# Grouped-query attention and a squared-ReLU FFN on one core: transposes moved from TensorE to DMA crossbar transposes

## The chip, the cores and the metric

The kernel runs on one core of a Trainium2 chip. The metric is the device time of one execution in microseconds (us), lower is better; the median of several runs is compared.

## The reference

Eight batches of attention with 16 query heads over 4 key/value heads (sequence 384, head size 64), then an FFN with a squared ReLU on the 3072 rows that come out:

```python
batch, n_q_heads, n_kv_heads, seq, head_dim = (8, 16, 4, 384, 64)
n_tokens, d_model, d_ff = (3072, 1024, 2048)
k = np.repeat(k, group, axis=1); v = np.repeat(v, group, axis=1)
scores = scale * np.matmul(q, k.transpose(0, 1, 3, 2))
attn = np.exp(scores - max); attn = attn / (np.sum(attn) + 1e-09)
x = np.matmul(attn, v).transpose(0, 2, 1, 3).reshape(B * S, H * D)
h = np.maximum(x @ w_in, 0.0)
out = (h * h @ w_out)
```

## The kernel before

Inputs are loaded as bf16 by POOL's DMA queue, one batch of k, v and q at a time, some two batches ahead; the FFN weights stay in SBUF. A batch has 8 pairs of heads (`NPB`), and p counts pairs over all batches, 64 in all. TensorE contracts over partitions, so q and k (which arrive with the sequence on partitions) must be turned to have the head size there, and the attention output must be turned to have the model dimension there. The kernel before does all of this on TensorE with an identity matrix, three 128x128 transposes to a group, into one PSUM buffer `pt`, which DVE copies out:

- `emit_kT(gi)` (L243): one group for each key head; k has first been doubled by a DVE copy (`emit_k`, into `k_dup`) so that two heads of a pair can use the two halves of the array.
- `emit_qT(p)` (L256): one group for each pair.
- `emit_oT(p)` (L308): one group for each pair, from `o_sb` into chunk c of `xT`, the FFN's input.

All four engines get their instructions from a recorder in the order in which the `emit_` functions are called; it works out the semaphore waits from what each operation reads and writes. Each engine runs its own list in order.

That order is a loop over steps n. A step does the scores of pair n (`emit_sc`, three times: two matmuls on halves of the array, then exp on ACT), the product with v of pair n-1 (`emit_av`, nine matmuls twice), its normalisation on DVE (`emit_norm`: reciprocal, multiply into `o_sb`), the kT and qT groups of pair n+2 and the oT group of pair n-1. Between these it calls `fill(ns)`, which takes FFN blocks of four matmuls from a generator until a credit is used up. The FFN of batch b may start once its last oT is recorded (`done_x`), so batch 0's attention runs without FFN work; from then on a batch's FFN has slightly more work than the slots of a batch take, so it falls back further with each batch, and the last FFN runs alone at the end. An FFN of a batch is 16 tiles of 8 up matmuls of 384 columns (L332; relu on DVE into `hr`, Square on ACT into `h2T`), then 6 tiles of 16 down matmuls of 512 columns (L352; copy on DVE into `y_sb`, store by SP's queue). The first half of an up tile reads chunks 0 to 3 of `xT`, the second chunks 4 to 7.

Of the kernel before, what the change touches and what calls it, by code (L numbers as in the profile page):

```python
# [5 lines left out]
ALU = mybir.AluOpType  # L6
# [4 lines left out]
class Recorder:  # L11
# [6 lines left out]
    def __init__(self, nc):  # L18
        self.nc = nc
        self.ops = []  # L20
        self.writer = {}
        self.readers = {}
        self.dma_sems = {}

    def add(self, eng, fn, reads=(), writes=(), dma=None):
        i = len(self.ops)
        deps = set()
        for r in reads:
            if r in self.writer:
                deps.add(self.writer[r])  # L30
        for w in writes:
            if w in self.writer:
                deps.add(self.writer[w])
            deps.update(self.readers.get(w, ()))
        raw = {self.writer[r] for r in reads if r in self.writer}
        for r in reads:
            self.readers.setdefault(r, []).append(i)
        for w in writes:
            self.writer[w] = i
            self.readers[w] = []  # L40
        need = set()
        for d in deps:
            o = self.ops[d]
            if o["dma"] is None and o["eng"] == eng and dma is None:
                if eng in self.IN_ORDER or d not in raw:
                    continue
            need.add(d)
        self.ops.append(dict(eng=eng, fn=fn, dma=dma, need=need, signal=False))
        return i

# [54 lines left out]
def bass_gqa_attention__then__ffn_squared_relu_kernel(  # L105
# [11 lines left out]
    B, H, S, D = 8, 16, 384, 64  # L117
    HKV = 4
    NJ = S // 128
    FF = 2048  # L120
    F = H * D
    NPB = H // 2
    NP = B * NPB
    NKC = F // 128
    NFC = FF // 128
    NST, NQT, NKT, NEX, NXT, NHR, NY = 3, 3, 2, 3, 3, 3, 3

    R = Recorder(nc)

    def sb(name, shape, dt=bf16):  # L130
        return nc.alloc_sbuf_tensor(name, shape, dt)

    ident = sb("ident", [128, 128])
    warm = sb("warm", [128, 512])
    q_st = [sb(f"q_st{i}", [128, H, NJ * D]) for i in range(NST)]
    k_st = [sb(f"k_st{i}", [128, HKV, NJ, D]) for i in range(NST)]
    k_dup = [sb(f"k_dup{i}", [128, HKV * NJ, 2, D]) for i in range(2)]
    v_st = [sb(f"v_st{i}", [128, HKV * NJ, D]) for i in range(NST)]
    v_aug = [sb(f"v_aug{i}", [128, HKV * NJ, D + 1]) for i in range(2)]
    kT = [sb(f"kT{i}", [128, S]) for i in range(NKT)]  # L140
    qT = [sb(f"qT{i}", [128, S]) for i in range(NQT)]
    expT = [sb(f"expT{i}", [128, NJ, 2 * S]) for i in range(NEX)]
    rinv = [sb(f"rinv{i}", [128, NJ, 2], f32) for i in range(2)]
    o_sb = [sb(f"o_sb{i}", [128, NJ, 2, D]) for i in range(2)]
    xT = [sb(f"xT{i}", [128, NKC, S]) for i in range(NXT)]
    w_in_sb = sb("w_in_sb", [128, NKC, FF])
    w_out_sb = sb("w_out_sb", [128, NFC, F])
# [4 lines left out]
    sc_ps = [nc.alloc_psum_tensor(f"sc_ps{i}", [128, 2, 512], f32) for i in range(2)]  # L152
    po = nc.alloc_psum_tensor("po", [128, 512], f32)
    pt = nc.alloc_psum_tensor("pt", [128, 1024], bf16)
    f_ps = [nc.alloc_psum_tensor(f"f_ps{i}", [128, 512], f32) for i in range(2)]
    po_v = po[:, 0:NJ * 2 * (D + 1)].rearrange("p (i s e) -> p i s e", i=NJ, s=2)


    def load_k(b):
        st = b % NST  # L160
        R.add("gpsimd", lambda g: g.dma_start(
            k_st[st].ap().rearrange("p g j d -> p g (j d)"),
            k[b].rearrange("g (p j) d -> p g (j d)", j=NJ)),
            writes=[("k_st", st)], dma=f"k{st}")
# [68 lines left out]
    def emit_v(b):  # L233
        R.add("vector", lambda e: e.tensor_copy(v_aug[b % 2][:, :, 0:D], v_st[b % NST][:, :, :]),
              reads=[("v_st", b % NST)], writes=[("v_aug", b % 2)])

    def emit_k(b):
        src = k_st[b % NST].ap().rearrange("p g j d -> p (g j) d").unsqueeze(2)
        R.add("vector", lambda e: e.tensor_copy(  # L239
            k_dup[b % 2][:, :, :, :], src.to_broadcast([128, HKV * NJ, 2, D])),  # L240
            reads=[("k_st", b % NST)], writes=[("k_dup", b % 2)])

    def emit_kT(gi):  # L243
        b, g = gi // HKV, gi % HKV

        def tr(pe):
            for j in range(NJ):
                src = k_dup[b % 2][:, g * NJ + j].rearrange("p x d -> p (x d)")
                m = pe.matmul(pt[:, j * 128:(j + 1) * 128], src, ident[:], is_transpose=True)  # L249
            return m  # L250

        R.add("tensor", tr, reads=[("k_dup", b % 2), "ident"], writes=["pt"])
        R.add("vector", lambda e: e.tensor_copy(kT[gi % NKT][:, :], pt[:, 0:S]),  # L253
              reads=["pt"], writes=[("kT", gi % NKT)])

    def emit_qT(p):  # L256
        b, c = p // NPB, p % NPB
        st = b % NST
        src = q_st[st][:, 2 * c:2 * c + 2, :].rearrange("p h e -> p (h e)")

        def tr(pe):
            for t in range(NJ):
                m = pe.matmul(pt[:, t * 128:(t + 1) * 128], src[:, t * 128:(t + 1) * 128], ident[:],  # L263
                              is_transpose=True)
            return m

        R.add("tensor", tr, reads=[("q_st", st, 2 * c), ("q_st", st, 2 * c + 1), "ident"], writes=["pt"])
        R.add("vector", lambda e: e.tensor_copy(qT[p % NQT][:, :], pt[:, 0:S]),  # L268
              reads=["pt"], writes=[("qT", p % NQT)])

    def emit_sc(p, j):
        gi, u = p // 2, (p * NJ + j) % 2

        def sc(pe):
            for x in range(2):
                rows = slice(64 * x, 64 * x + 64)
                m = pe.matmul(sc_ps[u][:, x, 0:S], kT[gi % NKT][rows, j * 128:(j + 1) * 128],  # L277
                              qT[p % NQT][rows, :])
            return m

        R.add("tensor", sc, reads=[("kT", gi % NKT), ("qT", p % NQT)], writes=[("sc", u)])
        src = sc_ps[u][:, :, 0:S].rearrange("p x (t c) -> p x t c", t=NJ)
        dst = expT[p % NEX][:, j, :].rearrange("p (t x c) -> p x t c", x=2, t=NJ)
        R.add("scalar", lambda e: e.activation(dst, src, AF.Exp, scale=0.125),  # L284
              reads=[("sc", u)], writes=[("expT", p % NEX, j)])
# [15 lines left out]
    def emit_norm(p):  # L301
        R.add("vector", lambda e: e.reciprocal(rinv[p % 2].ap().unsqueeze(3), po_v[:, :, :, D:D + 1]),  # L302
              reads=["po"], writes=[("rinv", p % 2)])
        rb = rinv[p % 2].ap().unsqueeze(3).to_broadcast([128, NJ, 2, D])
        R.add("vector", lambda e: e.tensor_tensor(o_sb[p % 2][:, :, :, :], po_v[:, :, :, 0:D], rb, ALU.mult),  # L305
              reads=["po", ("rinv", p % 2)], writes=[("o_sb", p % 2)])

    def emit_oT(p):  # L308
        b, c = p // NPB, p % NPB

        def tr(pe):
            for i in range(NJ):
                m = pe.matmul(pt[:, i * 128:(i + 1) * 128],  # L313
                              o_sb[p % 2][:, i].rearrange("p s d -> p (s d)"), ident[:], is_transpose=True)
            return m

        R.add("tensor", tr, reads=[("o_sb", p % 2), "ident"], writes=["pt"])
        R.add("vector", lambda e: e.tensor_copy(xT[b % NXT][:, c, :], pt[:, 0:S]),  # L318
              reads=["pt"], writes=[("xT", b % NXT, c)])

# [60 lines left out]
    def fill(ns):  # L381
        credit[0] += ns
        while credit[0] > 0:
            t = next(ffn, 0)
            if not t:
                credit[0] = 0.0
                return
            credit[0] -= t

    emit_k(0)  # L390
    emit_v(0)
    emit_kT(0)
    emit_qT(0)
    emit_qT(1)
    SLOT = 4900 / 7.0
    for n in range(NP + 2):
        live = n < NP
        if live:
            emit_sc(n, 0)
            fill(SLOT)  # L400
            emit_sc(n, 1)
            fill(SLOT)
        if 0 <= n - 1 < NP:
            emit_av(n - 1, 0)
            fill(SLOT)
            emit_av(n - 1, 1)
            emit_norm(n - 1)
            fill(SLOT)
        if live:
            emit_sc(n, 2)  # L410
            fill(SLOT)
        if n + 2 < NP:
            if (n + 2) % NPB == 0:
                bn = (n + 2) // NPB
                emit_k(bn)
                emit_v(bn)
                if bn + 2 < B:
                    load_k(bn + 2)
                    load_v(bn + 2)
                    load_q(bn + 2, 0)  # L420
            if (n + 2) % 2 == 0:
                emit_kT((n + 2) // 2)
                fill(SLOT / 2)
            emit_qT(n + 2)
            fill(SLOT)
        if 0 <= n - 1 < NP:
            emit_oT(n - 1)
            fill(SLOT)
            if n % NPB == 0:
                done_x[0] = n // NPB - 1  # L430
# [32 lines left out]
```

## Time and profile before

| | us |
|---|---|
| median of 3 runs | 517.85 (517.54 to 524.07) |
| the profiled execution | 519.5 |
| its span, first to last instruction | 517.7 |
| PE busy in it | 487.7 |
| DVE busy | 209.4 |
| ACT busy | 213.6 |

PE is TensorE's matmul stream, PEld its weight loads, DVE, ACT, POOL and SP the other engines. Matmuls overlap in the pipeline, so their mean duration is longer than the time that each adds; the chain of work that ended last counts from end to end. Times within the span count from its first instruction.

### The profile page before, as it was taken

To read this page: it belongs to the slowest core of one execution; us is meant where nothing else is said; L and a number is where in the kernel's file an instruction comes from. 1 tells how busy PE (TensorE), PEld (TensorE's weight loads), DVE (VectorE), ACT (ScalarE), POOL (GpSimd) and SP (SyncE) were. 2 spreads that over 40 slices of the span, in tenths; PEclk is the share of its full clock that TensorE was granted. 3 is DMA by queue.
4 is the path that set the end of the run, shared out by engine and by line. 5 is a ranking of instruction groups with operands and counts; after the bars stand their busy time and mean duration, and the time that the engine had idled before them with its cause. 6 is when DMAs were issued, how large, how long until landed. Compare 5 with 4: busy or idle time off the path is not lost.

```text
span 517.7 us, 8710 instructions
## 1 busy us (share of the span) xinstructions
PE 487.7 (94%) x3832; PEld 247.7 (48%) x3832; DVE 209.4 (40%) x483; ACT 213.6 (41%) x321; POOL 32.6 (6%) x43
## 2 busy tenths in 40 slices
PE   6879998999989999999999999989999999999997
PEld 3434554455534554445544545444554445545643
DVE  2443444345433444434443445324443344433421
ACT  2654552345532555335543355333553345601410
POOL 8720002000010000100000000000000000000000
PEclk8776999999999999999999999999999999999999
DMA  9999997310091001810051100011001110011012
GB/s 117 196 198 207 207 126 105 70 42 0 1 133 63 20 1 17 138 42 22 1 82 44 61 0 1 30 53 42 0 2 42 42 41 1 2 62 61 1 42 81
DMA packets 42358, 30.97 MB, mean 60 GB/s; under 512 B 25936, under 2 KB 34128, under 8 KB 42320
## 3 DMA queue, kind: packets, MB, share of 16 engines
q0 software_dynamic: 35408, 17.83, 26.4%
q1 hardware_dynamic: 6912, 12.59, 6.3%
q8 instruction: 30, 0.49, 0.4%
q14 instruction: 8, 0.07, 0.0%
HBM read 35.65 MB, written 12.58 MB: 93 GB/s over the span
## 4 chain that ended last, share of the span: by engine, by line
PE 90%; DVE 7%; issue 1%; DMA 1%; POOL 0%; ACT 0%; POOLq 0%
PE f_ps L332 33%; PE f_ps L352 33%; PE sc_ps L277 10%; PE po L294 8%; PE pt L313 3%; PE pt L263 3%; DVE hr L339 2%; DVE qT L268 2%; DVE kT L253 1%; PE pt L249 1%; DVE y_sb L360 1%; DVE o_sb L305 1%; DMA v_st<-in_v_dram 1%; DVE k_dup L239 0%; DVE rinv L302 0%
## 5 line engine op out<-in xcount | busy, mean ns | idle before, releaser
L284 ACT ACTIVATE expT<-sc_ps 128x768 bf16<-128x768 f32 x192 | 150.5, 804 | 149.4 <-PE sc_ps L277 148.9
L332 PE MATMUL f_ps<-xT,w_in_sb 128*128 128x384 bf16 x1024 | 203.6, 329 | 0.0
L352 PE MATMUL f_ps<-w_out_sb,h2T 128*128 128x512 bf16 x768 | 191.5, 380 | 0.0
L341 ACT ACTIVATE h2T<-hr 128x384 bf16<-128x384 f32 x128 | 66.9, 523 | 131.3 <-DVE hr L339 129.0
L332 PEld LDWEIGHTS f_ps<-xT,w_in_sb 128*128 128x128 bf16 x1024 | 86.5, 98 | 55.6 <-issue 13.8
L339 DVE TENSOR_SCALAR hr<-f_ps 128x384 f32<-128x384 f32 x128 | 71.2, 556 | 88.5 <-PE f_ps L332 88.5
L352 PEld LDWEIGHTS f_ps<-w_out_sb,h2T 128*128 128x128 bf16 x768 | 65.0, 97 | 66.2 <-issue 11.0
L360 DVE COPY y_sb<-f_ps 128x512 f32<-128x512 f32 x48 | 33.2, 692 | 84.2 <-PE f_ps L352 83.8
L277 PE MATMUL sc_ps<-qT,kT 64*128 64x384 bf16 x384 | 65.1, 348 | 0.9 <-ACT expT L284 0.6
L294 PEld LDWEIGHTS po<-v_aug,expT 128*128 128x128 bf16 x1152 | 52.2, 100 | 22.7 <-issue 4.7
L294 PE MATMUL po<-v_aug,expT 128*128 128x65 bf16 x1152 | 57.1, 197 | 0.0
L277 PEld LDWEIGHTS sc_ps<-qT,kT 64*128 64x128 bf16 x384 | 17.6, 94 | 59.0 <-issue 45.1
L302 DVE RECIPROCAL rinv<-po 128x6 f32<-128x6 f32 x64 | 12.4, 193 | 60.9 <-PE po L294 60.9
L305 DVE TENSOR_TENSOR o_sb<-po,rinv 128x384 bf16<-128x384 f32 x64 | 35.7, 557 | 2.2
L263 PE MATMUL pt<-ident,q_st 128*128 128x128 bf16 x192 | 22.3, 227 | 13.3 <-DVE kT L253 12.9
L318 DVE COPY xT<-pt 128x384 bf16<-128x384 bf16 x64 | 22.7, 355 | 24.7 <-PE pt L313 24.7
L268 DVE COPY qT<-pt 128x384 bf16<-128x384 bf16 x64 | 22.7, 355 | 24.6 <-PE pt L263 24.4
L313 PE MATMUL pt<-ident,o_sb 128*128 128x128 bf16 x192 | 22.1, 226 | 8.4 <-DVE qT L268 7.0
L263 PEld LDWEIGHTS pt<-ident,q_st 128*128 128x128 bf16 x192 | 13.8, 99 | 25.4 <-DVE kT L253 17.9
L313 PEld LDWEIGHTS pt<-ident,o_sb 128*128 128x128 bf16 x192 | 12.9, 99 | 25.0 <-DVE qT L268 20.1
L178 POOL DMA_DIRECT2D q_st<-in_q_dram x9 | 10.0, 1115 | 209.8 <-PE pt L263 209.8
L253 DVE COPY kT<-pt 128x384 bf16<-128x384 bf16 x32 | 11.4, 356 | 14.2 <-PE pt L249 14.0
(19 smaller groups left out, 60.7 us busy)
## 6 DMA issues: line engine op xcount, KB each, us to landing
out_dram<-y_sb SPq DMA_DIRECT2D x48, 256.0 KB, 2.0
q_st<-in_q_dram POOLq DMA_DIRECT2D x7, 768.0 KB, 9.8
w_in_sb<-in_moe_w_in_dram POOLq DMA_DIRECT2D x8, 512.0 KB, 17.8
w_out_sb<-in_moe_w_out_dram POOLq DMA_DIRECT2D x4, 1024.0 KB, 38.5
k_st<-in_k_dram POOLq DMA_DIRECT2D x8, 192.0 KB, 10.7
v_st<-in_v_dram POOLq DMA_DIRECT2D x8, 192.0 KB, 11.0
q_st<-in_q_dram POOLq DMA_DIRECT2D x1, 576.0 KB, 8.1
q_st<-in_q_dram POOLq DMA_DIRECT2D x1, 192.0 KB, 4.1
```

Of the source, the lines that this page charges most:

```text
L263: m = pe.matmul(pt[:, t * 128:(t + 1) * 128], src[:, t * 128:(t + 1) * 128], ident[:], is_transpose=True)
L268: R.add("vector", lambda e: e.tensor_copy(qT[p % NQT][:, :], pt[:, 0:S]), reads=["pt"], writes=[("qT", p % NQT)])
L277: m = pe.matmul(sc_ps[u][:, x, 0:S], kT[gi % NKT][rows, j * 128:(j + 1) * 128], qT[p % NQT][rows, :])
L284: R.add("scalar", lambda e: e.activation(dst, src, AF.Exp, scale=0.125), reads=[("sc", u)], writes=[("expT", p % NEX, j)])
L294: m = pe.matmul(po_v[:, i, s, :], expT[p % NEX][:, j, f * 128:(f + 1) * 128], v_aug[b % 2][:, g * NJ + j, :], start=(j == 0), stop=(j == N ...
L305: R.add("vector", lambda e: e.tensor_tensor(o_sb[p % 2][:, :, :, :], po_v[:, :, :, 0:D], rb, ALU.mult), reads=["po", ("rinv", p % 2)], wri ...
L313: m = pe.matmul(pt[:, i * 128:(i + 1) * 128], o_sb[p % 2][:, i].rearrange("p s d -> p (s d)"), ident[:], is_transpose=True)
L332: m = pe.matmul(f_ps[u][:, 0:S], w_in_sb[:, kc, c * 128:(c + 1) * 128], xT[b % NXT][:, kc, :], start=(kc == 0), stop=(kc == NKC - 1))
L339: R.add("vector", lambda e, u=u, r=r: e.tensor_scalar_max(hr[r][:, :], f_ps[u][:, 0:S], 0.0), reads=[("f_ps", u)], writes=[("hr", r)])
L341: R.add("scalar", lambda e, r=r, c=c: e.activation(h2T[b % 2][:, c, :], hr[r][:, :], AF.Square), reads=[("hr", r)], writes=[("h2T", b % 2, ...
L352: m = pe.matmul(f_ps[u][:, :], h2T[b % 2][:, c, i * 128:(i + 1) * 128], w_out_sb[:, c, jj * 512:(jj + 1) * 512], start=(c == 0), stop=(c = ...
L360: R.add("vector", lambda e, u=u, yb=yb, jj=jj: e.tensor_copy(y_sb[yb][:, jj * 512:(jj + 1) * 512], f_ps[u][:, :]), reads=[("f_ps", u)], wr ...
```

## The change

From batch 2 on (`DMA_QK = 2`) q and k, and from batch 1 on (`DMA_O = 1`) the attention output, are turned by DMA crossbar transposes issued by SP, from SBUF to SBUF, in place of TensorE groups and DVE copies. For each batch one transpose turns the whole of `k_dup` (128x1536) into `kTb`, and two turn the halves of `q_st` (128x1536 each) into `qTb`; they are issued in step n = 8b - 5, with the k copy, which moves there from step 8b - 2. Each pair's `o_sb` (128x384) is turned into its chunk of `xT` by a transpose recorded where the oT group was; `o_sb` has four buffers in place of two. A DMA also waits for the last one with the same semaphore. For batch 1 the v copy now stands ahead of the k copy. The calls of `fill` stay as they are.

```diff
+        if dma is not None:
+            if dma in self.dma_last:
+                need.add(self.dma_last[dma])
+            self.dma_last[dma] = i
...
+    DMA_QK, DMA_O = 2, 1
+    NST, NQT, NKT, NEX, NXT, NHR, NY, NO = 3, 3, 2, 3, 3, 3, 3, 4
...
+    qTb = [sb(f"qTb{i}", [128, NPB, S]) for i in range(2)]
+    kTb = [sb(f"kTb{i}", [128, HKV, S]) for i in range(2)]
...
+    def emit_turn(b):
+        R.add("sync", lambda e: e.dma_start_transpose(
+            kTb[b % 2].ap().rearrange("p g (j c) -> p (g j) c", j=NJ),
+            k_dup[b % 2].ap().rearrange("p a x d -> p (a x d)")),
+            reads=[("k_dup", b % 2)], writes=[("kTb", b % 2)], dma=f"kt{b % 2}")
+        for part in range(2):
+            cs = slice(4 * part, 4 * part + 4)
+            R.add("sync", lambda e, cs=cs: e.dma_start_transpose(
+                qTb[b % 2][:, cs, :].rearrange("p h (t c) -> p (h t) c", t=NJ),
+                q_st[b % NST][:, 2 * cs.start:2 * cs.stop, :].rearrange("p h e -> p (h e)")),
+                reads=[("q_st", b % NST, h) for h in range(2 * cs.start, 2 * cs.stop)],
+                writes=[("qTb", b % 2, part)], dma=f"qt{b % 2}_{part}")
...
     def emit_kT(gi):
         b, g = gi // HKV, gi % HKV
+        if b >= DMA_QK:
+            return
...
     def emit_qT(p):
         b, c = p // NPB, p % NPB
+        if b >= DMA_QK:
+            return
...
+        if b >= DMA_QK:
+            kt, kt_key = kTb[b % 2][:, c // 2, :], ("kTb", b % 2)
+            qt, qt_key = qTb[b % 2][:, c, :], ("qTb", b % 2, c // 4)
...
     def emit_oT(p):
         b, c = p // NPB, p % NPB
+        if b >= DMA_O:
+            R.add("sync", lambda e: e.dma_start_transpose(
+                xT[b % NXT][:, c, :].rearrange("p (i c) -> p i c", i=NJ),
+                o_sb[p % NO].ap().rearrange("p i s d -> p (i s d)")),
+                reads=[("o_sb", p % NO)], writes=[("xT", b % NXT, c)], dma=f"xt{p % 8}")
+            return
...
         if n + 2 < NP:
+            if (n + 5) % NPB == 0 and n + 5 >= DMA_QK * NPB:
+                emit_k((n + 5) // NPB)
+                emit_turn((n + 5) // NPB)
             if (n + 2) % NPB == 0:
                 bn = (n + 2) // NPB
-                emit_k(bn)
                 emit_v(bn)
+                if bn < DMA_QK:
+                    emit_k(bn)
```

## Rows read from the trace of the kernel before

**Rows 1.** The page: engines' busy time, and the granted clock in 40 slices.

```profile
PE 487.7 (94%) x3832; PEld 247.7 (48%) x3832; DVE 209.4 (40%) x483; ACT 213.6 (41%) x321; POOL 32.6 (6%) x43
...
PEclk8776999999999999999999999999999999999999
```

**Rows 2.** The page: the chain that ended last, by line.

```profile
PE f_ps L332 33%; PE f_ps L352 33%; PE sc_ps L277 10%; PE po L294 8%; PE pt L313 3%; PE pt L263 3%; DVE hr L339 2%; DVE qT L268 2%; DVE kT L253 1%; PE pt L249 1%; DVE y_sb L360 1%; DVE o_sb L305 1%; DMA v_st<-in_v_dram 1%; DVE k_dup L239 0%; DVE rinv L302 0%
```

**Rows 3.** The chain in order of time, 200 to 232: start, us, what.

```profile
202.40 0.17 PE pt L263 x3
202.56 0.86 PE f_ps L352 x4
...
203.60 0.27 PE sc_ps L277 x2
203.87 0.97 PE f_ps L352 x4
...
206.07 0.28 PE po L294 x9
...
225.25 0.34 PE pt L313 x3
```

**Rows 4.** The chain in order of time, 455 us to the end.

```profile
459.25 13.81 PE f_ps L352 x64
473.06 20.80 PE f_ps L332 x128
```

**Rows 5.** Groups of PE, 107 to 459: count, busy us, mean ns, idle before.

```profile
L332 PE MATMUL f_ps<-xT,w_in_sb 128*128 128x384 bf16 x768 | 155.1, 327 | 0.0
L352 PE MATMUL f_ps<-w_out_sb,h2T 128*128 128x512 bf16 x515 | 132.7, 380 | 0.0
L277 PE MATMUL sc_ps<-qT,kT 64*128 64x384 bf16 x280 | 46.4, 333 | 0.0
L294 PE MATMUL po<-v_aug,expT 128*128 128x65 bf16 x864 | 42.4, 194 | 0.0
L313 PE MATMUL pt<-ident,o_sb 128*128 128x128 bf16 x143 | 16.0, 221 | 3.2 <-DVE qT L268 2.0
L263 PE MATMUL pt<-ident,q_st 128*128 128x128 bf16 x135 | 15.0, 220 | 7.5 <-DVE kT L253 7.5
L249 PE MATMUL pt<-ident,k_dup 128*128 128x128 bf16 x66 | 7.3, 220 | 1.7 <-DVE k_dup L239 1.7
```

**Rows 6.** Groups of PE, 50.3 to 107.

```profile
L352 PE MATMUL f_ps<-w_out_sb,h2T 128*128 128x512 bf16 x95 | 24.5, 380 | 0.0
L332 PE MATMUL f_ps<-xT,w_in_sb 128*128 128x384 bf16 x104 | 21.1, 327 | 0.0
L277 PE MATMUL sc_ps<-qT,kT 64*128 64x384 bf16 x44 | 7.4, 333 | 0.0
L294 PE MATMUL po<-v_aug,expT 128*128 128x65 bf16 x126 | 6.1, 194 | 0.0
L313 PE MATMUL pt<-ident,o_sb 128*128 128x128 bf16 x24 | 2.7, 221 | 1.5 <-DVE qT L268 1.3
```

**Rows 7.** Groups by line, whole span: the v copy.

```profile
L234 DVE COPY v_aug<-v_st 128x768 bf16<-128x768 bf16 x8 | 2.9, 359 | 2.1 <-DMA v_st<-in_v_dram 2.1
```

**Rows 8.** The page: SP's DMA queue (packets, MB, share), its issues (us to landing).

```profile
q1 hardware_dynamic: 6912, 12.59, 6.3%
...
out_dram<-y_sb SPq DMA_DIRECT2D x48, 256.0 KB, 2.0
```

**Rows 9.** The q loads: POOL's timeline (batch 2's issue), and landing times.

```profile
17.98 1.29 POOL L178 DMA_DIRECT2D q_st<-in_q_dram  x1
...
DMA to landing us min/median/max: 4.1/8.6/43.3
```

**Rows 10.** The timeline, 100 to 109: start, us, engine, what.

```profile
101.62 0.56 DVE L305 TENSOR_TENSOR o_sb<-po,rinv 128x384 bf16<-128x384 f32 x1
...
108.69 0.49 PE L332 MATMUL f_ps<-xT,w_in_sb 128*128 128x384 bf16 x2
```

More of the change, by code (lines that the diff above doesn't have):

```diff
@@ L23, in __init__ @@
         self.dma_sems = {}
+        self.dma_last = {}
     def add(self, eng, fn, reads=(), writes=(), dma=None):
@@ L125, in bass_gqa_attention__then__ffn_squared_relu_kernel @@
     NFC = FF // 128
-    NST, NQT, NKT, NEX, NXT, NHR, NY = 3, 3, 2, 3, 3, 3, 3
+    DMA_QK, DMA_O = 2, 1
+    NST, NQT, NKT, NEX, NXT, NHR, NY, NO = 3, 3, 2, 3, 3, 3, 3, 4
     R = Recorder(nc)
@@ L141, in bass_gqa_attention__then__ffn_squared_relu_kernel @@
     qT = [sb(f"qT{i}", [128, S]) for i in range(NQT)]
+    qTb = [sb(f"qTb{i}", [128, NPB, S]) for i in range(2)]
+    kTb = [sb(f"kTb{i}", [128, HKV, S]) for i in range(2)]
     expT = [sb(f"expT{i}", [128, NJ, 2 * S]) for i in range(NEX)]
     rinv = [sb(f"rinv{i}", [128, NJ, 2], f32) for i in range(2)]
-    o_sb = [sb(f"o_sb{i}", [128, NJ, 2, D]) for i in range(2)]
+    o_sb = [sb(f"o_sb{i}", [128, NJ, 2, D]) for i in range(NO)]
     xT = [sb(f"xT{i}", [128, NKC, S]) for i in range(NXT)]
@@ L272, in emit_sc @@
         gi, u = p // 2, (p * NJ + j) % 2
+        b, c = p // NPB, p % NPB
+        if b >= DMA_QK:
+            kt, kt_key = kTb[b % 2][:, c // 2, :], ("kTb", b % 2)
+            qt, qt_key = qTb[b % 2][:, c, :], ("qTb", b % 2, c // 4)
+        else:
+            kt, kt_key = kT[gi % NKT], ("kT", gi % NKT)
+            qt, qt_key = qT[p % NQT], ("qT", p % NQT)
         def sc(pe):
@@ L276, in sc @@
                 rows = slice(64 * x, 64 * x + 64)
-                m = pe.matmul(sc_ps[u][:, x, 0:S], kT[gi % NKT][rows, j * 128:(j + 1) * 128],
-                              qT[p % NQT][rows, :])
+                m = pe.matmul(sc_ps[u][:, x, 0:S], kt[rows, j * 128:(j + 1) * 128], qt[rows, :])
             return m
-        R.add("tensor", sc, reads=[("kT", gi % NKT), ("qT", p % NQT)], writes=[("sc", u)])
+        R.add("tensor", sc, reads=[kt_key, qt_key], writes=[("sc", u)])
         src = sc_ps[u][:, :, 0:S].rearrange("p x (t c) -> p x t c", t=NJ)
@@ L304, in emit_norm @@
         rb = rinv[p % 2].ap().unsqueeze(3).to_broadcast([128, NJ, 2, D])
-        R.add("vector", lambda e: e.tensor_tensor(o_sb[p % 2][:, :, :, :], po_v[:, :, :, 0:D], rb, ALU.mult),
-              reads=["po", ("rinv", p % 2)], writes=[("o_sb", p % 2)])
+        R.add("vector", lambda e: e.tensor_tensor(o_sb[p % NO][:, :, :, :], po_v[:, :, :, 0:D], rb, ALU.mult),
+              reads=["po", ("rinv", p % 2)], writes=[("o_sb", p % NO)])
     def emit_oT(p):
         b, c = p // NPB, p % NPB
+        if b >= DMA_O:
[4 more added lines that the diff above has]
+            return
         def tr(pe):
@@ L313, in tr @@
                 m = pe.matmul(pt[:, i * 128:(i + 1) * 128],
-                              o_sb[p % 2][:, i].rearrange("p s d -> p (s d)"), ident[:], is_transpose=True)
+                              o_sb[p % NO][:, i].rearrange("p s d -> p (s d)"), ident[:], is_transpose=True)
             return m
-        R.add("tensor", tr, reads=[("o_sb", p % 2), "ident"], writes=["pt"])
+        R.add("tensor", tr, reads=[("o_sb", p % NO), "ident"], writes=["pt"])
         R.add("vector", lambda e: e.tensor_copy(xT[b % NXT][:, c, :], pt[:, 0:S]),
```

## The prediction

> **What bounds the kernel now.** The page comes first: PE is busy for 94% of the span, DVE for 40%, ACT for 41%, and the clock row stays at 9 from the seventh slice to the end [rows 1]. Next the chain of work that ended last, by line: the two FFN matmul lines carry two thirds of it, scores and attention-times-values 18%, and the three transpose lines (L249, L263, L313) with the DVE copies that empty `pt` most of what is left [rows 2]. So whatever is taken out of PE's own order moves the end, and work on other engines counts only where PE waits for it.
>
> Then the chain piece by piece in a steady stretch, for unit prices measured end to end (the mean of one matmul on the page contains its pipeline latency and must not be multiplied) [rows 3]: three transposes between two FFN blocks 0.17 us; a pair of score matmuls 0.27; nine value matmuls 0.28; four FFN matmuls 0.86 after a transpose or a value group, but 0.97 after scores, so scores cost 0.27 + 0.11 = 0.38. The row at 225.25 shows the other side of a transpose: with no FFN block before it the group takes 0.34, because `pt` is one buffer and its DVE copy must end first. The pure FFN at the end gives the remaining units, with nothing else in the way [rows 4]: 20.80 / 128 = 0.1625 us for an up matmul, 13.81 / 64 = 0.216 for a down matmul.
>
> Last, counts of each kind in the two stretches that the change touches, with the idle time ahead of each [rows 5, 6]. All of PE's idle time from 107 to 459 us stands ahead of transposes: 3.2 + 7.5 + 1.7 = 12.4 us.
>
> **What is removed.** By the loop, TensorE loses 8 x 6 = 48 qT groups, 4 x 6 = 24 kT groups and 8 x 7 = 56 oT groups, three transposes each: 128 of 160 groups. DVE loses as many copies.
>
> *107 to 459 us* (here every transpose goes): the other work is 768 x 0.1625 + 515 x 0.216 + 140 x 0.38 + 96 x 0.28 = 124.8 + 111.2 + 53.2 + 26.9 = 316.1 us [rows 3 to 5]. The stretch lasts 352.0, so transposes and what they make PE wait for cost **35.9 us**. A cross-check: 344 transposes are 115 groups, 115 x 0.17 = 19.5; idle 12.4; the remaining 4 is the pipeline running empty before each wait (the 0.34 against 0.17).
>
> *50.3 to 107 us* (steps 9 to 16, 56.7 us): 104 x 0.1625 + 95 x 0.216 + 22 x 0.38 + 14 x 0.28 = 49.7 us, so 7.0 us of excess [rows 3, 4, 6]. Here qT(12) to qT(15), kT(6) and kT(7) stay on PE: 6 x 0.17 = 1.0, and a stall in the two steps that have a kT; (35.9 - 19.5) / 48 steps = 0.34 a step, so 0.7. Saved: 7.0 - 1.7 = **5.3 us**. After 459 us only FFN is left [rows 4]; before 50 us nothing is removed.
>
> **What is added or moved on the engines.** For batch 1 `emit_v` now comes ahead of `emit_k`, in a stretch where the chain runs through the kT transpose: one v copy later, **0.36 us** lost [rows 7]. For batches 2 to 7 the k copy runs three steps earlier on a DVE that is idle over half of the time. The slots between attention steps are still filled by the same calls, so PE's order of the remaining work is unchanged.
>
> **What is added on SP and the DMA engines.** Per batch three transposes of 128x1536 and eight of 128x384: 36 + 24 = 60 blocks of 128x128. No row shows a crossbar transpose. Below: the store on the same queue moves 256 KB and lands in 2.0 us [rows 8], so 32 KB at its rate take 0.25 us. Above, if each source row of 256 bytes is one packet: the SP queue's 6912 packets took 6.3% of 16 engines' 517.7 us, 75 ns each [rows 8]; 128 x 75 ns / 16 = 0.6 us a block. Further off, a whole landing of 2.0 us for each block (the slow rival). A gain below zero is not possible from an added transfer. I take 0.25 to 0.6, since the store is on the same queue: 15 to 36 us of the queue in a batch. PE's new batch is 316.1 / 48 x 8 = 52.7 us, so the queue keeps up, and its price on the path is nothing as long as three covers hold:
>
> - The q and k transposes of batch b are issued in step 8b-5 and first read in step 8b: 5 steps of 6.6 us (316.1 / 48) = 33 us. 36 blocks at 0.6 and the 15 blocks of the oT issued in between are 31 us: tight at the upper bound only. For batch 2 the issue is at about 50.3 + 2 x 7.1 = 64.5 us; its q load was issued at 18 us and no q load took over 43.3 us to land [rows 9], so it is there by 61.
> - The last oT of batch 1: `o_sb` is ready at 101.62 + 0.56 = 102.2 us, and the FFN half that reads chunks 4 to 7 starts at 108.69 [rows 10]: 6.5 us, some 5.5 with PE's gains in between. Three blocks at 0.6 plus 2.0 for landing are 3.8 us. Later batches have more room, since the FFN falls further behind. If this cover fails, PE stands still at the head of the FFN for the difference, at most seven times.
> - SP issues in order. Queued behind a waiting transpose are the y stores (three `y_sb` buffers, each filled again a batch later) and the next oT; DVE's `norm` now waits for the transpose of four steps before, 26 us. POOL's q loads wait for crossbar transposes in place of PE's, a batch ahead of use.
>
> With the stalls on `pt` gone, what is late next is PE itself: ACT is busy 41% of the span and DVE 40% [rows 1], and DVE loses copies.
>
> [...]
>
> **The sum.** 35.9 + 5.3 - 0.4 = 40.8 us. The profiled execution took 519.5 us (span 517.7, 1.8 around it): 478.7 after. It stood 1.65 us above the median of 517.85, so the forecast for the median is **477 us**, -7.9%.
>
> **Rivals.**
> *The stalls move instead of going* (the DVE copies that PE waited for queue behind `hr` and `y_sb` copies and `norm`; exp or Square may take their place). Only the groups' own time is then won: 128 x 0.17 = 21.8, **496 us**. For it: `hr`, `norm` and exp still empty the banks that PE fills. Against: all of PE's idle is ahead of transposes [rows 5], and each score and FFN bank has a second buffer.
> *The crossbar is the bound, slower than before.* One queue turns one block at a time, c us each. It keeps up to c = 52.7 / 60 = 0.88. Beyond, from 64.5 us on it has 15 blocks of batch 1, 6 x 36 for q and k and 6 x 24 for oT: 375, and behind the last the final FFN, 20.8 + 96 x 0.216 = 41.5 us, and a store's 2.0: the end is at 108 + 375c. That passes the time before at c = 1.09; at a store's full landing per block, 2.0, it is **858 us**. For it: nothing shown excludes a serial crossbar. Against: stores of 128 rows of 2 KB land whole in those 2.0 us.
> [...]
>
> **Chances and range.** All stalls gone 0.78 (own range 472 to 487: a few us at the FFN heads, or units that come out a little better); stalls move 0.13; crossbar the bound 0.07 (slower); a gain mostly eaten by late landings 0.02 (no change). Two per cent is about what a measurement of this kernel can tell from no change, and both first cases are beyond it: faster 0.91, same 0.02, slower 0.07. The range 471 to 491 leaves out the slow rival and most of the second.
>
> **What would show it.** No idle time on PE after about 90 us; transposes of q and k landing well ahead of step 8b; the FFN's first half following the previous batch's last store at once; SP's time from `o_sb` to landing under 5 us; PE's pieces 0.86 and 0.97 unchanged (a slower one would mean that crossbar traffic disturbs PE's reads). Wrong it would be by a wait of PE for `kTb`, `qTb` or `xT`, or DVE waiting at L305 for a transpose.

## The result, and the profile after

The changed kernel takes 478.9 us at the median (477.49 to 481.75), the kernel before 520.96 in the runs beside it: a ratio of 0.920, 95% interval 0.910 to 0.929. The forecast was 477, range 471 to 491. The profiled execution has a span of 475.7 us against 517.7; the forecast for the span was 476.9.

Up to the first FFN tile (steps 0 to 8, where the kernels do nearly the same) the granted TensorE clock is 0.50 of full speed for a varying share of the time (in the kernel before its mean is 0.51 from 10 to 20 us, 1.00 from 20 to 30 and 0.67 from 30 to 40; with only the output by crossbar 0.54, 0.50 and 0.50), so that stretch takes 37 to 48 us by chance and design together; profiles are therefore compared below from the first FFN up matmul to the end of the span. That matmul is here, in the profile before and in the one after (timeline: start, us, engine, what; line numbers are those of each kernel's own file):

```profile
43.03 2.74 PE L332 MATMUL f_ps<-xT,w_in_sb 128*128 128x384 bf16 x8
43.50 2.74 PE L369 MATMUL f_ps<-xT,w_in_sb 128*128 128x384 bf16 x8
```

So 475.7 - 43.5 = 432.2 us are left after it; in the kernel before 517.7 - 43.0 = 474.7.

Where did 42.5 us go? Between the starts of the FFN's batches (first up matmul of each, from the same timeline): batch 0 to 1 took 64.7 us and takes 58.9; batch 1 to 6 took 310.3 and takes 277.4; from there to the end 99.7 and 95.9. The gain is spread over all batches that still have attention, and nothing is given back at the end.

The groups of PE in the steady part, 107 to 420 us (count, busy us, mean ns, idle before), answer to [rows 5]:

```profile
L369 PE MATMUL f_ps<-xT,w_in_sb 128*128 128x384 bf16 x752 | 143.3, 327 | 0.0
L389 PE MATMUL f_ps<-w_out_sb,h2T 128*128 128x512 bf16 x504 | 126.4, 380 | 1.8 <-issue 0.9
L309 PE MATMUL sc_ps<-qTb,kTb 64*128 64x384 bf16 x276 | 45.7, 332 | 0.0
L325 PE MATMUL po<-v_aug,expT 128*128 128x65 bf16 x846 | 41.5, 194 | 0.0
```

The transposes are gone from the list, and with them the idle time. The 1.8 us at L389 are not a wait: this profile lacks the records of some matmuls (504 of L389 against 527 weight loads in the same stretch). A second profile of the same kernel ("changed, again" below) has them, and its row has no idle time:

```profile
L389 PE MATMUL f_ps<-w_out_sb,h2T 128*128 128x512 bf16 x526 | 129.5, 380 | 0.0
```

By the unit prices of [rows 3, 4] its work is 751 x 0.1625 + 526 x 0.216 + 138 x 0.38 + 94 x 0.28 = 314.4 us, in a stretch of 313: within half a per cent, nothing else is left. The kernel before had 316 in 352. PE's pieces are unchanged as well: from 200 to 215 us four FFN matmuls take 0.86 us, or 0.97 after scores, as before.

What PE waited for in the whole span (us in total, times, longest):

```profile
PE pt L288 <- DVE kT L276: 4.5, 6, 2.2
PE pt L350 <- DVE qT L293: 3.6, 8, 0.5
PE f_ps L389 <- issue: 1.3, 8, 0.2
PE pt L272 <- DVE k_dup L247: 1.2, 1, 1.2
...
PE f_ps L369 <- DMA xT<-o_sb: 0.6, 1, 0.6
```

The rows with `pt` are batches 0 and 1, which still turn on TensorE; the row with "issue" is the missing records again. The last is the one wait that the change added from the first FFN on. It stands at the head of the FFN of batch 1, and the chain of work that ended last goes through it (start, us, what):

```profile
97.20 0.82 PE f_ps L389 x3
98.02 0.02 issue
98.04 0.70 DVE y_sb L397
98.75 0.02 issue
98.76 0.33 SPq L401
99.09 0.04 issue
99.14 4.92 DMA xT<-o_sb
104.06 0.05 issue
104.10 0.82 PE f_ps L369 x4
```

Read it backwards: the second half of the first up tile waits for the last chunk of `xT`; its transpose was issued at 99.14, only after a y store that stood ahead of it in SP's order had had its DVE copy; it took 4.9 us to land, beside a q load (issued at 86.8, landed 16.2 us later). The cover of some 5.5 us was overrun by 0.6.

The new work on the DMA side (packets, MB, share of 16 engines; issues, median us to landing):

```profile
q0 software_dynamic: 35408, 17.83, 29.0%
q1 hardware_dynamic: 63136, 26.36, 24.8%
...
q_st<-in_q_dram POOLq DMA_DIRECT2D x7, 768.0 KB, 16.2
...
xT<-o_sb SPq DMA_TRANSPOSE x56, 2.4
...
qTb<-q_st SPq DMA_TRANSPOSE x14, 4.9
...
kTb<-k_dup SPq DMA_TRANSPOSE x7, 4.3
```

Against [rows 8], SP's queue has 56,224 more packets. Their time is 24.8% x 16 x 475.7 - 522 = 1366 us of engine time, 24 ns each; for 7 x 36 + 56 x 3 = 420 blocks that is 3.25 us of one engine or 0.20 us of all sixteen. q loads land in 16.2 us at the median where they took 9.8, which PE does not wait for in the steady part.

### The profile page after: what moved, and what is told of

Read it like the earlier page. It is cut to its first block, busy times and chain, and to the rows that moved or that the text cites. A ratio compares the mean times of both kernels' runs of the same rounds, so it can differ in the third digit from the quotient of the medians.

```text
span 475.7 us, 7922 instructions
## 1 busy us (share of the span) xinstructions
PE 457.2 (96%) x3419; PEld 228.6 (48%) x3448; DVE 167.3 (35%) x356; ACT 213.0 (45%) x321; POOL 32.6 (7%) x43
## 3 DMA queue, kind: packets, MB, share of 16 engines
q1 hardware_dynamic: 63136, 26.36, 24.8%
## 4 chain that ended last, share of the span: by engine, by line
PE 93%; DMA 3%; DVE 2%; issue 1%; POOL 1%; SPq 0%; POOLq 0%
PE f_ps L369 37%; PE f_ps L389 35%; PE sc_ps L309 10%; PE po L325 8%; DMA q_st<-in_q_dram 2%; DMA xT<-o_sb 1%; PE pt L288 1%; PE pt L350 1%; DVE qT L293 1%; DVE o_sb L336 0%; DVE kT L276 0%; PE pt L272 0%; DVE y_sb L397 0%; POOL k_st L169 0%; DVE rinv L333 0%
## 5 line engine op out<-in xcount | busy, mean ns | idle before, releaser
L369 PE MATMUL f_ps<-xT,w_in_sb 128*128 128x384 bf16 x1024 | 194.1, 328 | 0.6 <-DMA xT<-o_sb 0.6
L389 PE MATMUL f_ps<-w_out_sb,h2T 128*128 128x512 bf16 x739 | 180.9, 380 | 2.4 <-issue 1.3
L369 PEld LDWEIGHTS f_ps<-xT,w_in_sb 128*128 128x128 bf16 x1024 | 88.9, 98 | 63.9 <-issue 13.8
L389 PEld LDWEIGHTS f_ps<-w_out_sb,h2T 128*128 128x128 bf16 x768 | 66.5, 97 | 76.3 <-issue 11.6
L309 PE MATMUL sc_ps<-qTb,kTb 64*128 64x384 bf16 x288 | 47.7, 332 | 0.0
L309 PEld LDWEIGHTS sc_ps<-qTb,kTb 64*128 64x128 bf16 x288 | 13.5, 93 | 49.9 <-issue 33.5
L336 DVE TENSOR_TENSOR o_sb<-po,rinv 128x384 bf16<-128x384 f32 x64 | 35.7, 557 | 2.2
L309 PE MATMUL sc_ps<-qT,kT 64*128 64x384 bf16 x96 | 17.3, 393 | 0.9 <-ACT expT L315 0.6
L288 PE MATMUL pt<-ident,q_st 128*128 128x128 bf16 x48 | 6.3, 249 | 5.5 <-DVE kT L276 4.5
L169 POOL DMA_DIRECT2D k_st<-in_k_dram x8 | 6.5, 809 | 65.3 <-DVE k_dup L247 64.5
L309 PEld LDWEIGHTS sc_ps<-qT,kT 64*128 64x128 bf16 x96 | 4.1, 97 | 11.1 <-issue 6.4
L288 PEld LDWEIGHTS pt<-ident,q_st 128*128 128x128 bf16 x48 | 3.3, 105 | 8.8 <-DVE kT L276 6.6
L293 DVE COPY qT<-pt 128x384 bf16<-128x384 bf16 x16 | 5.7, 354 | 4.4 <-PE pt L288 4.1
## 6 DMA issues: line engine op xcount, KB each, us to landing
q_st<-in_q_dram POOLq DMA_DIRECT2D x7, 768.0 KB, 16.2
```

The costliest lines, as they stand in the source:

```text
L309: m = pe.matmul(sc_ps[u][:, x, 0:S], kt[rows, j * 128:(j + 1) * 128], qt[rows, :])
L336: R.add("vector", lambda e: e.tensor_tensor(o_sb[p % NO][:, :, :, :], po_v[:, :, :, 0:D], rb, ALU.mult), reads=["po", ("rinv", p % 2)], wr ...
L369: m = pe.matmul(f_ps[u][:, 0:S], w_in_sb[:, kc, c * 128:(c + 1) * 128], xT[b % NXT][:, kc, :], start=(kc == 0), stop=(kc == NKC - 1))
L389: m = pe.matmul(f_ps[u][:, :], h2T[b % 2][:, c, i * 128:(i + 1) * 128], w_out_sb[:, c, jj * 512:(jj + 1) * 512], start=(c == 0), stop=(c = ...
```

## The experiments

All medians below are device times; "from the FFN" is the span of the profile less the start of its first up matmul, "from the FFN of batch 1" the same from the first up matmul of the next batch.

| kernel | median us | first up matmul | from the FFN | from the FFN of batch 1 |
|---|---|---|---|---|
| before | 521 | 43.0 | 474.7 | 410.0 |
| changed | 478.9 | 43.5 | 432.2 | 373.3 |
| only the output by crossbar | 506.9 | 48.4 | 459.4 | 398.3 |
| only q and k by crossbar | 492.7 | 48.2 | 442.4 | 380.8 |
| changed, PE groups back without copies | 501.8 | 42.1 | 452.6 | 391.6 |
| before, kT moved away from qT | 503.9 | 37.4 | 460.5 | 399.5 |
| turn in step 8b-2 | 491.7 | 47.5 | 440.2 | 382.2 |
| turn in step 8b-1 | 525.0 | 47.3 | 477.4 | 410.7 |
| four transposes for one | 497.2 | 47.9 | 450.8 | 392.1 |
| six transposes for one | 633.7 | 41.4 | 590.9 | 514.8 |
| early output too | 480.7 | 44.7 | 435.5 | 377.2 |
| changed, kT moved | 476.8 | 41.2 | 433.5 | 376.9 |
| changed, again | 479.2 | 43.4 | 432.2 | 373.2 |

The last column is there because the half clock can reach past the first up matmul. In the kernel before it lasts until 47.0 us and in the changed one until 47.2; with the PE groups back, and with kT moved in the kernel before, it has ended by then (the first eight up matmuls take 1.47 and 1.48 us, not 2.74). The rows show what that is worth (busy times as below, then the clock and DMA): first the kernel before, then the changed kernel with PE groups back.

```profile
43.00:47.00 4.00, 4.00 (x15) 1.55 (x14) 0.62 (x2) 1.41 (x3) 0.00 (x0) 0.50 1.13 212
42.00:46.00 4.00, 4.00 (x41) 2.42 (x40) 1.28 (x4) 2.03 (x3) 0.00 (x0) 1.00 1.12 212
```

So "from the FFN" flatters a kernel whose half clock has ended before it by up to 2 us.

**Own time or waits?** The theory is that a transpose group costs PE 0.17 us of its own, and that the other half of the gain is PE waiting for the one buffer `pt`. To separate them, groups go back on TensorE with nobody to copy them out:

```diff
+    def idle_group():
+        def tr(pe):
+            for i in range(NJ):
+                m = pe.matmul(pt[:, i * 128:(i + 1) * 128], ident[:], ident[:], is_transpose=True)
+            return m
+        R.add("tensor", tr, reads=["ident"], writes=["pt"])
...  in emit_kT, emit_qT and emit_oT, ahead of each new return:
+            idle_group()
```

> The changed kernel with 128 groups of three transposes of the identity put back on TensorE at the old places; they are written to pt and never copied out, so nothing waits for DVE. Theory: only the groups' own time comes back, 128 x 0.17 = 21.8 us: 500 to 501 us; the rest of the way to the time before, some 19 us, is waits on pt. Rival (the whole 41 us is TensorE's transpose time, its DVE copies being hidden): 515 us or more. Rival (PE has slack now): 480 us.

Measured: 501.8 us (496.5 to 503.0), and 452.6 from the FFN, 20.4 more than the changed kernel. That difference is a little small, since this kernel starts its FFN at full clock. From the FFN of batch 2 to that of batch 6, at full clock and without a wait in either kernel, 82 groups cost 235.2 - 221.4 = 13.8 us: 0.17 a group, 21.5 for all 128. The groups of PE in its stretch from 107 to 430 have this row:

```profile
L267 PE MATMUL pt<-ident 128*128 128x128 bf16 x336 | 34.5, 220 | 0.0
```

No idle time stands ahead of them. So some 21 us of the 42.5 are the transposes' own time, and the other 21 came with the copies. Of these, 13.9 us stand in the trace of the kernel before as idle time of PE ahead of transposes (from 43 us on); that the rest is the pipeline running empty before each wait is argued from the 0.34 against 0.17 of [rows 3]. Both halves of the theory hold; the two rivals fall.

**The waits by themselves.** If half of the gain is a collision on one buffer, some of it can be had without any DMA. In the kernel before, the kT group moves away from the qT group that follows it:

```diff
             emit_sc(n, 1)
+            if n + 2 < NP and (n + 2) % 2 == 0:
+                emit_kT((n + 2) // 2)
             fill(SLOT)
...
             if (n + 2) % 2 == 0:
-                emit_kT((n + 2) // 2)
                 fill(SLOT / 2)
...  emit_k, emit_v and the loads move up behind emit_sc(n, 0)
```

> The kernel before, all transposes on TensorE, with one thing moved: the kT group (and, once a batch, the k and v copies and the loads ahead of it) stands behind the second scores of its step in place of directly ahead of the qT group, so that the two no longer meet on the one pt buffer. Nothing is removed. Theory (waits on pt are worth some 22 of the 42 us, those of kT with qT and of the k copy with kT 11 us of idle time and more in drained pipeline): 8 to 14 us less from the first FFN tile to the end, 461 to 467 of 474.7, about 505 to 510 us in all. Rival (PE would wait for something else, the matmuls themselves are the bound): 474 from the first FFN tile, no change.

Measured: ratio 0.967 to the kernel before (0.959 to 0.975), 460.5 us from the FFN, 14.2 less with every instruction kept. Some 2 of the 14.2 are the clock at the start; from the FFN of batch 1 on, with both at full clock, it is 10.5. What PE waits for between 107 and 450 us is now one row; compare the 12.4 us of [rows 5]:

```profile
PE pt L313 <- DVE qT L268: 2.0, 4, 0.9
```

So the moved group took away most of the waits. Two `pt` buffers, the direct test, were not tried.

**One part at a time.** The change's two constants undo one part each:

```diff
-    DMA_QK, DMA_O = 2, 1
+    DMA_QK, DMA_O = 8, 1    # only the output
+    DMA_QK, DMA_O = 2, 8    # only q and k
```

> Only the attention output is turned by the crossbar; all q and k groups are back on TensorE. Theory (a group's own 0.17 us plus waits on the one pt buffer): 72 groups come back, 72 x 0.17 = 12.2 us, and the pairs kT then qT still collide on pt, which I put at half to most of the 15.9 us of waits: 479 + 12 + 8 to 13 = 499 to 504 us, with PE idle ahead of L263's successor only. Rival (only the groups' own time counts, the waits were covered by other work): 491 us.

Measured: 506.9 us and 459.4 from the FFN, 27.2 more than the changed kernel; 72 groups of 0.17 are 12 of it and waits most of the other 15, above the 8 to 13 expected (up to 1.7 us are a stretch at half clock, 150.7 to 154.1). Between 107 and 450 us:

```profile
PE pt L288 <- DVE kT L276: 7.5, 13, 0.9
PE pt L272 <- DVE k_dup L247: 2.8, 4, 1.5
```

The 7.5 us are the same as in [rows 5]: taking oT off `pt` does nothing for the collision of kT with qT. The expectation of 499 to 504 is missed by 3 us, less than the opening took longer in the profiled run (48.4 against 43.5).

> Only q and k are turned by the crossbar; all oT groups are back on TensorE, one to a step, with nothing else on pt from step 14 on. Theory: 56 x 0.17 = 9.5 us and no wait, since the copy of one step is long done in the next: 488 us, no PE idle time ahead of the oT groups. Rival (each group keeps its share of the 40 us, 0.31 us): 479 + 17 = 496 us.

Measured: 492.7 us (484.5 to 493.7), and 442.4 from the FFN: 10.2 more than the changed kernel for 56 groups, 0.18 each. The expected 488 lies inside the range of the runs; the median misses it by 5 us, and the profiled run's opening was as much longer (48.2). In the stretch from 107 to 430:

```profile
L350 PE MATMUL pt<-ident,o_sb 128*128 128x128 bf16 x144 | 15.9, 220 | 0.1
```

One group to a step hardly ever waits. The two parts left out one at a time cost 10.2 and 27.2, together 37.4, and both left out 42.5. I read the last 5 us as waits of oT for qT's copy, which either part takes away ([rows 5] has 2.0 us of them as idle time); that is argued, not shown.

**How much cover do q and k need?** The turn is issued later:

```diff
-            if (n + 5) % NPB == 0 and n + 5 >= DMA_QK * NPB:
-                emit_k((n + 5) // NPB)
-                emit_turn((n + 5) // NPB)
+            if (n + 1) % NPB == 0 and n + 1 >= DMA_QK * NPB:    # and n + 2
+                emit_k((n + 1) // NPB)
+                emit_turn((n + 1) // NPB)
```

> The k copy and the three transposes of q and k are issued in step 8b-1 in place of 8b-5. What is left between their issue and the first score of the batch is the tail of one step, some 2.5 us. Theory (measured in the changed kernel: 1.4 us of SP's queue for k, then 4.9 us until the first half of q has landed): PE waits 3.5 to 6 us at the head of batches 2 to 7, 20 to 35 us in all: 500 to 515 us, and the wait stands ahead of the scores, put down to the transposes. Rival (the transposes are so cheap that the place doesn't matter): 479 us. Rival (the crossbar needs the 0.6 us a block of my upper bound, 14 us until the first half of q): 550 us.

Measured: 525.0 us, above the 500 to 515 expected, and 477.4 from the FFN. PE's waits:

```profile
PE sc_ps L309 <- DMA qTb<-q_st: 33.3, 6, 7.6
```

That is six heads at 5.5 us, inside the 20 to 35 expected. But the kernel lost 45.2 us, 12 more than the wait. The stretches around the head of batch 4 tell why (us, busy times of PE, PEld, DVE, ACT, POOL, then the granted clock and DMA):

```profile
220.00:227.00 7.00, 0.62 (x3) 0.10 (x1) 0.00 (x0) 0.00 (x0) 1.50 (x2) 0.77 1.17 190
227.00:233.00 6.00, 4.73 (x19) 1.59 (x20) 0.12 (x1) 1.62 (x2) 1.15 (x1) 0.50 0.63 115
233.00:238.00 5.00, 5.00 (x36) 2.28 (x33) 1.44 (x4) 0.81 (x1) 0.00 (x0) 0.89 1.39 203
238.00:243.00 5.00, 5.00 (x42) 2.41 (x41) 1.33 (x3) 2.43 (x3) 0.00 (x0) 1.00 0.18 62
```

PE stood idle for 7.6 us until 228.3; the granted clock was 0.50 from 227 to 233, 0.89 on the mean of the next 5 us and 1.00 from 238 on. By the two middle rows the matmuls that came back ran at half clock for nearly 6 us, which cost almost 3 us at this head. Over all six heads PE is busy for 26.9 us at half clock, a loss of some 13, which accounts for the 12.

> The same transposes issued in step 8b-2, one step of 6.7 us earlier than in the run before, so some 9 us of cover. Theory: k and the first half of q need 6.3 us, or more where loads are under way; they fit: 479 to 481 us, no wait of PE ahead of the scores but for batch 2, whose transposes run beside the weight loads or shortly after. Rival (0.6 us a block): PE waits some 8 us in each of six batches, 525 us.

Measured: 491.7 us where 479 to 481 was expected, and 440.2 from the FFN, 8.0 more than the changed kernel. PE's waits that are new:

```profile
PE f_ps L369 <- DMA xT<-o_sb: 5.6, 3, 3.1
PE sc_ps L309 <- issue: 2.7, 3, 1.0
```

The second row is the scores at the heads of batches 2, 3 and 4 (0.7, 1.0 and 0.9 us); it names no releaser, but each begins 0.1 us after the first half of q has landed, 8.3 to 9.4 us after the k transpose was issued. Only the first of the three was expected. What the expectation left out is SP's order. PE waits 3.1, 2.1 and 0.3 us for `xT` at the FFN heads of batches 1, 2 and 3, since three large transposes now stand shortly ahead of the last outputs of a batch (SP's timeline):

```profile
88.19 1.86 SPq L252 DMA_TRANSPOSE kTb<-k_dup  x1
90.09 6.20 SPq L258 DMA_TRANSPOSE qTb<-q_st  x2
96.33 1.26 SPq L342 DMA_TRANSPOSE xT<-o_sb  x1
```

So step 8b-5 is early less for the scores' sake than to keep the turn out of the way of the chunk that the next FFN waits for.

**Where does the queue become the bound?** Each output's transpose is followed by copies of itself into buffers that nobody reads:

```diff
                 reads=[("o_sb", p % NO)], writes=[("xT", b % NXT, c)], dma=f"xt{p % 8}")
+            for a in range(3):    # 5 in the second kernel
+                R.add("sync", lambda e, a=a: e.dma_start_transpose(
+                    jx[3 * (p % 2) + a].ap().rearrange("p (i c) -> p i c", i=NJ),
+                    o_sb[p % NO].ap().rearrange("p i s d -> p (i s d)")),
+                    reads=[("o_sb", p % NO)], writes=[("jx", p % 2, a)], dma=f"jx{p % 2}_{a}")
```

> Each transpose of an attention output is followed by three copies of itself into buffers that nobody reads: 8 x 4 = 32 of 128x384 in a batch beside the three large ones, 132 blocks for 60. Theory (the queue is held by SP for 1.2 us for each of them, 32 x 1.2 + 5.1 + 6 stores x 0.33 = 45 us of a batch of 53): hidden, 478 to 482 us. Rival (the crossbar or the DMA engines, not SP, set the rate, with the changed kernel near their limit): over 500 us.

Measured: 497.2 us, 450.8 from the FFN, 18.6 more: not hidden.

```profile
PE f_ps L375 <- DMA xT<-o_sb: 14.2, 3, 9.8
```

The three waits for `xT` stand at the FFN heads of batches 1, 2 and 3 (9.8, 3.7 and 0.8 us). From batch 4 on there is none, so the rate just suffices: SP's issues take 50 to 55 us of each later batch of 52 to 60, with hardly a gap, where the expectation had 45 of 53. Its silence on the start was wrong. SP is busy with batch 2's turn beside the loads of the opening until 84 us and then catches up slowly: the last chunk of batch 1 is issued at 115.1 us, in the changed kernel at 99.1.

> The same with five copies: 48 of 128x384 in a batch, 180 blocks. Theory: SP's hold of 1.2 us each makes 48 x 1.2 + 5.1 + 2 = 65 us of a batch, over PE's 53, so SP's queue becomes the bound: 50 + 7 x 65 + 43.5 = 530 to 555 us, PE waiting for xT. Rival (the hold is only the record of an issue, and transposes overlap): 480 us.

Measured: 633.7 us. The bound is SP, as expected; the time is 79 us beyond the range given. A step of SP in the middle of the run:

```profile
346.19 1.19 SPq L343 DMA_TRANSPOSE xT<-o_sb  x1
347.44 6.43 SPq L348 DMA_TRANSPOSE jx<-o_sb  x5
353.92 1.05 SPq L407 DMA_DIRECT2D out_dram<-y_sb  x2
355.01 1.21 SPq L343 DMA_TRANSPOSE xT<-o_sb  x1
```

355.0 - 346.2 = 8.8 us: back to back, a transpose holds SP for 1.29 us, not 1.2, and a store for half a microsecond. With the turn a batch is 73 to 80 us (the distance of the FFN heads, 65 expected), PE waits for `xT` seven times (119.0 us in all), and the mean clock over the span is 0.876, against 0.975 in the changed kernel.

**Do more of it.** In batch 0 no FFN covers the transposes, so the change seems to stop short:

```diff
-        if b >= DMA_O:
+        if b >= DMA_O or c < 5:
```

> The first five pairs of batch 0 also have their output turned by the crossbar. In that stage no FFN stands between the transposes, and the oT group with its wait is on the chain at 0.5 us and more a step. Theory: 2 to 4 us less than the changed kernel, 475 to 477, if the transposes, issued beside the saturated weight loads, land before the FFN of batch 0 starts at 43 us. Rival (they land late, 10 us and more beside the loads): PE waits at the first FFN tile, 479 to 484 us.

Measured: 480.7 us, ratio 0.923 to the kernel before (0.919 to 0.927), against 0.920 (0.910 to 0.929) for the changed kernel: no gain. The rival was nearer, with another victim:

```profile
PE pt L288 <- DVE kT L276: 4.2, 5, 2.2
PE pt L288 <- DMA q_st<-in_q_dram: 4.0, 2, 3.0
PE f_ps L369 <- DMA xT<-o_sb: 3.0, 1, 3.0
```

PE waits 3.0 us for batch 1's q load (not at all in the changed kernel) and as long at the head of the FFN of batch 1 (0.6 there). That the crossbar traffic delays these transfers is argued from the two rows, not shown by itself.

**Both.** The moved kT group should help the changed kernel's first two batches as well:

> The changed kernel with the kT groups that it still has (batches 0 and 1) moved apart from the qT groups as in the run before, the k copy of batch 1 ahead of the v copy again, and without the turn of a batch that doesn't exist. Theory: the 4.5 us that PE waits for kT's copy in the first 75 us go, part of them at half clock: 2 to 5 us less than the changed kernel, 473 to 477 us. Rival (in the opening the attention's own chain of scores, exp and values takes the place of that wait): 479 us.

Its edit is that of the moved kT group on top of the change, with the k copy ahead of the v copy and the guard `DMA_QK * NPB <= n + 5 < NP`.

> The changed kernel as it is, on the same chip, for comparison with the run before: 477 to 482 us, as it measured.

Measured on one chip: 476.8 us (476.1 to 478.7) and 479.2 (477.0 to 480.9); ratios to the kernel before 0.917 (0.913 to 0.921) and 0.921 (0.917 to 0.926). The fastest version here by its median, but the intervals overlap, so a gain is not shown. Its first up matmul comes 2.2 us earlier, and 1.3 of that is given back: PE's wait for `xT` at the FFN of batch 1 grows from 0.6 to 2.7 us.

## Why the prediction was right

**The sum.** By its own stretches: 50.3 to 107 us, forecast 5.3, measured 5.8 (64.7 to 58.9 from FFN 0 to FFN 1). The steady stretch, forecast 35.9 with everything after, measured 32.9 + 3.8 = 36.7. The swap of the v and k copies, forecast 0.36, and all else ahead of the FFN came to 0.5. Together 42.0 of span for a forecast of 40.8. Counting the work by unit prices and calling the rest removable was right because the rest was removable: by the same prices nothing of the 313 us is left over.

**Its two parts.** The groups' own time was put at 21.8 and measured some 21.5 with the groups put back (0.17 a group); the waits are what is left, 41.2 - 21.8 = 19.4 by the forecast and 42.5 - 21.5 = 21 by the runs.

**The rival of moved stalls** falls: no engine took DVE's place, and PE's idle time in the steady part went from 12.4 us to none.

**The price of a block.** The bounds of 0.25 and 0.6 us were made from the store's landing and its 75 ns per packet. A transpose packet took 24 ns, so the DMA engines need 0.20 us, below the lower bound. What holds the queue is SP, and by the instruction more than by the block: at least 1.18 us for three blocks, 1.27 for twelve (1.20, and 1.43 for k and 1.96 for q, at the median). The forecast of 15 to 36 us of queue in a batch is 8 x 1.2 + 1.4 + 2 x 1.9 = 15, for a reason that the prediction did not name; that it falls on the lower end of the range is luck.

From issue to landing, three blocks take 2.4 us at the median, and the 36 of a batch's turn, where no load is under way, 7.5 to 8.4 us from the first issue. What one block alone takes, no run here shows.

**The slow rival** is real in kind, and its place was named wrongly: the bound is SP's hold of each instruction and not the crossbar's time for a block. Small transposes back to back come to 1.29 / 3 = 0.43 us a block, and those of the turn to 0.23 at most (8.4 / 36). The hold decides between 32 small transposes in a batch, which a steady batch just hides, and 48, which it does not; the change has 8.

**The covers.** The first, 33 us for q and k, is 29 in the trace (issue at 120.1, first score at 149.0): the turn stands at the end of its step. The need was put at up to 31. It is 7.5 to 10.4 us from batch 3 on and 22 for batch 2, beside the loads of the opening (issued at 64.3, landed at 86.3, with the first half of q at 81.4 and the first score at 94.0), so the verdict held with room. The second was the tight one, and its need was too low: 3.8 us forecast for the last chunk, 6.1 measured from `o_sb` to landing, since a store stood ahead on SP (1.2 us) and the landing took 4.9 beside a q load, not 2.0 plus the blocks' time. It failed by 0.6 us, once, so the sign "under 5 us to landing" failed too; the longest landing of all, 10.5 us, ended 7 us ahead of its FFN. The third held: DVE never waits at L336.

**Slips of reading.** The clock row is at 9 from the fifth slice on, not the seventh. The prediction counted six turns; there are seven. The loop's guard lets step 59 turn a ninth batch that does not exist, on stale data. Nobody waits for it.

## What to carry to other kernels

When one engine is the bound, multiply its instruction counts by end-to-end prices from a stretch where they run undisturbed; what is left over is what an edit can win, and here about half of a transpose's cost was the wait on its single buffer, and more than a quarter of the whole gain was to be had by moving one call. A transfer that is hidden on average is settled at its latest consumer: look for what stands ahead of it in its queue's order and what else moves at that moment, and price its landing beside that traffic (here 4.9 us beside a q load, 2.3 alone). An added wait of several microseconds on TensorE can cost more than itself: here 33 us of them, in six pieces, cost 45, since PE was busy for 26.9 us around them at half clock.

## What was not expected of the hardware

- A crossbar transpose holds SP for 1.18 us or more where a store takes 0.33, not much more for 128x1536 (1.27 at least) than for 128x384 (1.18), and up to 5.7 us for 128x1536 beside the loads of the opening.
- The same 128x384 transpose lands in 2.3 us alone, in 8.2 to 9.6 beside the loads of the opening (50 to 86 us) and in up to 10.5 beside a q load of 768 KB (issued at 196.2).
- After 7.6 us of idle PE the clock was granted at 0.50 until 233, nearly 5 us more, and at 0.89 on the mean of the next 5, although the matmuls came back at once (turn in step 8b-1).
